# Reading part of the SSM kernel in natural layout and transposing it on PE, with DMA transposes kept for two of four segments

## The chip, the cores and the metric

The kernel runs on one core of one Trainium2 chip. The metric is the device time of one execution in microseconds (us), lower is better. Each kernel is executed several times, and most executions of a kernel agree within a per cent. Runs that are over 1.5% above the fastest of the same kernel are called slow and left out of ratios. A ratio is the mean time of one kernel's fast runs over the mean of the other's fast runs of the same rounds, so it is not quite the ratio of the medians that are quoted.

The engines are PE (matmuls), PEld (its weight loads), DVE (vector), ACT (scalar), POOL, and SP, which here only issues DMAs. The profile is one execution taken with the hardware profiler; L335 is line 335 of the program.

## The reference, cut to what matters

```python
h  = x + ln(x) * (causal_conv(kv, ssm_k) + kv * ssm_D)   # kv = shift4(k) * v
h2 = h + swiglu(ln(h))                                    # D = 640, F = 1728, S = 2048
```

The convolution over 2048 positions is done in four segments of 512. Segment p of the SSM kernel (640 channels by 512 taps) must lie with the taps on the partitions, so that PE can multiply it with a basis WG (the "G transform"). In memory `ssm_k` is `[640, 2048]`, channels first: the segment has to be transposed. D is added to tap 0.

## The kernel before

The parts that matter (`...` marks cuts). `load` and `add` enter an operation into a plan; a list scheduler then fixes the order of all engines, and each engine runs its own list strictly in that order.

```python
def gload(p, pr):            # segment p, transposed on its way in, on the SP queue
    add("SP", 2.7, lambda: nc.sync.dma_start_transpose(gT[p], A_ssm_k[:, p*MB:(p+1)*MB]), w=[f"gT{p}"], pr=pr, kb=640)
gload(0, -90)
...
add("DVE", 0.2, lambda: nc.vector.tensor_add(gT[0][0:1, 0, :], gT[0][0:1, 0, :], drow), ...)   # D

def front_tile(n, q, pr):    # k (640 KB) and v of one row tile, SP queue, then products on DVE
    load("SP", kd[:], run(r0 - 3, P), ...)
    load("SP", vb[:], vv[r0:r0 + P, :], ...)
    add("DVE", ..., lambda: nc.vector.tensor_mul(kd[:], kd[:], w4[:]), ...)
    ...

load("ACT", v of segment 0); load("ACT", WG); load("SP", k of segment 0)
g_transform(0, 9); front(0, 0)
gload(1, -30); gload(2, -20); ...; gload(3, -10)
x_transform(0, 8); pair(0, 0, 10, "first"); inverse(0, 20); ...
```

Names used below. PSUM is the memory that the matmuls write (psA and psF are its buffers); an eviction copies a result out of it. WG, WX and WI are constant bases. Front n makes kv of segment n (for segment 0 from whole-segment loads, for the others from `front_tile`). The X transform is the same as the G transform for kv; some of its results are evicted from PSUM by DVE. A pair is the complex product of one X and one G on DVE (six or eight 128x2560 operations of 1.48 us). Ten pairs, then per segment an inverse transform, a layer norm, a DMA transpose of the result (hT) and the FFN on PE.

## Time and profile before

309.1 us (median of 4 runs, 307.3 to 310.6). The profiled execution has a span of 309.8 us.

| stretch | us | what is full |
|---|---|---|
| head, to the first pair product | 0 to 41.2 | DMA engines |
| pairs of all segments | 41.2 to 240.9 | DVE (194.3 of 199.7 busy), PE nearly |
| last inverse, norm, hT | 240.9 to 258.7 | a chain over PE, ACT, DVE, POOL, DMA |
| last FFN | 258.7 to 309.8 | PE |

The table of windows shows these four stretches: start and end, its length, then busy time (and instructions) of PE, PEld, DVE, ACT and POOL, the granted PE clock, the busy share of the DMA engines, and GB/s.

```profile
41.20:240.90 199.70, 192.59 (x1128) 109.72 (x1126) 194.31 (x249) 128.37 (x249) 98.55 (x56) 0.98 0.56 146
240.90:258.70 17.80, 12.51 (x89) 7.99 (x86) 9.46 (x19) 8.39 (x18) 2.99 (x8) 0.93 0.27 65
258.70:309.80 51.10, 47.41 (x247) 23.99 (x247) 9.25 (x18) 16.54 (x28) 0.00 (x0) 0.96 0.28 75
```

Stretch 2 has DVE idle for 199.70 - 194.31 = 5.4 us only. So what starts DVE's full stretch earlier shortens the kernel, if PE can follow.

The head, in the timeline (start us, length us, engine, line, operation, result and source, count; in brackets the idle time before it and what ended it; SPq and ACTq are the issuing of DMAs):

```profile
1.23 22.30 SPq L276 DMA_TRANSPOSE wd<-in_A_ssm_k_dram  x3
...
1.67 0.45 ACTq L266 DMA_DIRECT2D hT<-in_A_v_dram  x1
...
15.34 1.23 PE L353 MATMUL psF<-hT,perm 128*128 128x320 bf16 x4 [4.07 <-DMA hT<-in_A_v_dram]
...
18.66 0.48 DVE L292 TENSOR_TENSOR wd<-wd,xln 1x640 bf16<-1x640 bf16 x1 [8.33 <-DMA wd<-in_A_ssm_k_dram]
...
23.57 5.35 SPq L276 DMA_TRANSPOSE hT<-in_A_ssm_k_dram  x1
...
25.36 3.42 PE L301 MATMUL psF<-wd,s 128*128 128x320 bf16 x24
...
27.27 0.82 DVE L373 TENSOR_TENSOR kv<-kv,rev 128x1280 bf16<-128x1280 bf16 x1
...
30.15 0.95 SPq L266 DMA_DIRECT2D k<-in_A_k_dram  x2
...
36.95 1.49 DVE L318 TENSOR_TENSOR k<-k,w 128x2560 bf16<-128x2560 bf16 x1 [3.79 <-DMA k<-in_A_k_dram]
38.35 0.82 DVE L388 CAST s<-psA 128x640 bf16<-128x640 f32 x1
...
39.23 1.22 PE L383 MATMUL psA<-kv,WX 128*128 128x320 bf16 x4 [3.38 <-DVE s L388]
...
41.22 1.48 DVE L393 TENSOR_TENSOR s<-s,s 128x2560 bf16<-128x2560 bf16 x1
```

The four transposes keep the SP queue from 1.23 to 28.92 us. Three things are late: v of segment 0 (15.3), the D add (18.7), and front 1's k loads, issued at 30.15 and 30.73.

### The profile page before, as it was taken

The page shows a single profiled execution, that of the slowest core. Times are in us where ns is not written, and L with a number is a line of the kernel's source. Part 1 is how long each engine was busy: PE and PEld are TensorE (multiplying, and loading weights), DVE is VectorE, ACT ScalarE, POOL GpSimd, SP SyncE. Part 2 cuts the span into 40 slices and gives each one's busy share as a digit, 9 for nine tenths or more (in the row PEclk, how much of TensorE's full clock was granted, in tenths as well). Part 3 has the DMA queues.
Part 4 walks back from the last instruction along what each step waited for, and adds up shares of the span by engine and source line. Part 5 has one row for each costly group of instructions (what it writes and reads, how often), then busy time and mean ns, then how long its engine had stood idle before and what let it go on. Part 6 is the DMA issues. An engine that isn't in the chain of part 4 may idle for free. (4 is left out here: it accounts for less than half of the span.)

```text
span 309.8 us, 4323 instructions
## 1 busy us (share of the span) xinstructions
PE 278.8 (90%) x1606; PEld 157.8 (51%) x1606; DVE 229.8 (74%) x302; ACT 166.1 (54%) x315; POOL 102.0 (33%) x70
## 2 busy tenths in 40 slices
PE   3389699999899998999997999999998975999995
PEld 1157457766454544655543556555455642444563
DVE  0354489999999999999996999999999660212112
ACT  5014459689775588026984491389761370555300
POOL 0000016545799936300897052049400030000000
PEclk9999969999999999999999799999999995999999
DMA  7999960639736329957363479464462032455011
GB/s 207 192 187 264 341 165 3 212 51 292 242 95 161 85 63 271 251 204 212 85 168 68 131 213 144 109 182 112 118 150 74 22 82 47 124 137 142 2 43 42
DMA packets 71769, 44.11 MB, mean 142 GB/s; under 512 B 30594, under 2 KB 69827, under 8 KB 71620
## 3 DMA queue, kind: packets, MB, share of 16 engines
q1 hardware_dynamic: 70112, 40.23, 51.7%
q10 hardware_dynamic: 1636, 3.61, 4.3%
q8 instruction: 12, 0.20, 0.3%
q14 instruction: 9, 0.07, 0.1%
HBM read 35.97 MB, written 2.62 MB: 125 GB/s over the span
## 5 line engine op out<-in xcount | busy, mean ns | idle before, releaser
L464 POOL TENSOR_SCALAR sm<-sm 128x1 f32<-128x1 f32 x32 | 56.6, 1769 | 149.2 <-ACT junk L461 142.1
L551 PE MATMUL psF<-hT,wg 128*128 128x512 bf16 x280 | 70.7, 384 | 7.7 <-DMA hT<-hl 6.8
L551 PE MATMUL psF<-hT,wu 128*128 128x512 bf16 x260 | 65.7, 384 | 0.0
L574 PE MATMUL psF<-wd,tT 128*128 128x320 bf16 x448 | 64.8, 299 | 0.8 <-ACT uc L563 0.5
L574 PEld LDWEIGHTS <-tT 128*128 128x128 bf16 x448 | 41.6, 97 | 23.7 <-issue 7.1
L556 ACT ACTIVATE sg<-psF 128x512 bf16<-128x512 f32 (+1 forms) x56 | 33.4, 597 | 27.6 <-PE psF L551 25.8
L551 PEld LDWEIGHTS <-wg 128*128 128x128 bf16 x280 | 27.5, 99 | 40.1 <-issue 10.1
L393 DVE TENSOR_TENSOR T<-s,s 128x2560 bf16<-128x2560 bf16 x32 | 47.0, 1481 | 1.0 <-ACT s L304 1.0
L393 DVE TENSOR_TENSOR s<-s,T 128x2560 bf16<-128x2560 bf16 x32 | 47.2, 1481 | 0.1
L565 DVE TENSOR_TENSOR tT<-sg,uc 128x512 bf16<-128x512 bf16 (+1 forms) x56 | 23.3, 416 | 30.7 <-ACT uc L563 30.7
L465 POOL TENSOR_TENSOR sm<-sm,mhalf 128x1 f32<-128x1 f32 x32 | 44.9, 1404 | 2.7
L563 ACT CAST uc<-psF 128x512 bf16<-128x512 f32 (+1 forms) x56 | 32.7, 585 | 17.9 <-PE psF L551 17.4
L551 PEld LDWEIGHTS <-wu 128*128 128x128 bf16 x260 | 25.6, 99 | 29.8 <-issue 1.4
L301 PEld LDWEIGHTS <-s 128*128 128x128 bf16 x256 | 25.9, 101 | 12.2 <-issue 0.8
L304 ACT CAST s<-psF 128x640 bf16<-128x640 f32 x32 | 21.9, 691 | 17.4 <-PE psF L301 17.3
L301 PE MATMUL psF<-wd,s 128*128 128x320 bf16 x192 | 29.9, 314 | 0.0
L383 PE MATMUL psA<-kv,WX 128*128 128x320 bf16 x128 | 20.7, 304 | 3.4 <-DVE s L388 3.4
L488 PE MATMUL psA<-s,WI 128*128 128x320 bf16 x128 | 20.2, 315 | 3.7 <-DVE s L393 3.6
L461 ACT ACTIVATE junk<-x,sm 128x640 bf16<-128x640 bf16 x28 | 23.4, 835 | 0.2
L579 DVE TENSOR_TENSOR o<-psF,x 128x640 bf16<-128x640 f32 x16 | 13.1, 816 | 14.0 <-PE psF L574 14.0
L460 ACT ACTIVATE junk<-x 128x640 bf16<-128x640 bf16 x28 | 20.7, 741 | 3.4 <-DVE x L511 3.0
L388 ACT CAST s<-psA 128x640 bf16<-128x640 f32 x29 | 18.9, 706 | 4.6 <-PE psA L383 4.6
(51 smaller groups left out, 222.8 us busy)
## 6 DMA issues: line engine op xcount, KB each, us to landing
k<-in_A_k_dram SPq DMA_DIRECT2D x12, 640.0 KB, 5.3
wg<-in_B_w_gate_dram SPq DMA_DIRECT2D x24, 320.0 KB, 3.1
wu<-in_B_w_up_dram SPq DMA_DIRECT2D x24, 320.0 KB, 3.7
out_dram<-o SPq DMA_DIRECT2D x16, 160.0 KB, 1.8
wd<-in_B_w_down_dram SPq DMA_DIRECT2D x1, 2080.0 KB, 9.5
v<-in_A_v_dram SPq DMA_DIRECT2D x12, 160.0 KB, 4.9
x<-in_A_q_dram SPq DMA_DIRECT2D x3, 640.0 KB, 5.1
s<-const_wg ACTq DMA_DIRECT2D x1, 1024.0 KB, 15.4
```

Source lines behind the costliest of these rows:

```text
L301: nc.tensor.matmul(ps(g)[:, h, 0:NH], WG[:, kt, ct * P:(ct + 1) * P], gT[p][:, kt, h * NH:(h + 1) * NH], start=(kt == 0), stop=(kt == 3))
L304: add("ACT", act(D), lambda g=g, ct=ct: nc.scalar.copy(r3(G[p][ct // 4][:, ct % 4, :]), ps(g)[:, :, 0:NH]), r=[g], w=[Gk[p] + "cs"[ct // 4 ...
L383: nc.tensor.matmul(ps(g)[:, h, 0:NH], WX[:, kt, ct * P:(ct + 1) * P], kv[:, base + kt, h * NH:(h + 1) * NH], start=(kt == 0), stop=(kt == 1))
L393: add("DVE", dve(n * D), lambda: f(o, a, b), r=ks(ak) + ks(bk), w=ks(ok), after=["WG0", "WG1"] if ok[:2] == "s7" else [], pr=pr)
L461: add("ACT", act(D) + 0.45, lambda: nc.scalar.activation(junk[:], src, ACT.Square, bias=s[:, 0:1], accum_out=s[:, 1:2]), r=[xk, k + "a"], ...
L464: e.tensor_scalar(s[:, 3:4], s[:, 1:2], 1.0 if vec else 1.0 / D, EPS, op0=ALU.mult, op1=ALU.add)
L465: e.tensor_tensor(s[:, 4:5], s[:, 3:4], mhalf[:], op=ALU.pow)
L551: i = nc.tensor.matmul(ps(gr)[:, which, :], w[:, kt, cc * P:(cc + 1) * P], hT[b][:, kt, :], start=(kt == 0), stop=(kt == 4))
L556: apart(gr, 0, nc.scalar.activation(sg[s][:z, :], ps(gr)[:z, 0, :], ACT.Silu))
L563: add("ACT", act(MB), lambda gr=gr, s=s, z=z, merged=merged: nc.scalar.copy(uc[s][:z, :], ps(gr)[64:128, 0, :] if merged else ps(gr)[:, 1, ...
L565: add("DVE", dve(MB), lambda c=c, s=s, z=z: TM(tT[:z, c * MB:(c + 1) * MB], sg[s][:z, :], uc[s][:z, :]), r=[f"sg{s}", f"uc{s}"], w=[f"tT{c ...
L574: nc.tensor.matmul(ps(gr)[:, h, 0:NH], tT[:z, c * MB + m * P:c * MB + (m + 1) * P], wd[:z, c, h * NH:(h + 1) * NH], start=(c == 0), stop=( ...
```

## The change

Its intent: take the slow DMA transposes away from the front. Segments 0 and 1 are loaded as they lie in memory (into buffers of the FFN that are still unused) and transposed on PE by matmuls with an identity; D is added by one-row matmuls into the same PSUM; ACT evicts. Segments 2 and 3 keep their DMA transposes, planned at 28 us or later. The diff also replaces the order pass. Cut to its core:

```diff
-    def gload(p, pr):
-        add("SP", 2.7, lambda: nc.sync.dma_start_transpose(gT[p], ...), ...)
-    gload(0, -90)
+    def gload(p, pr, q="SP"):
+        if p in TRANS:                                   # TRANS = {2: 28, 3: 28}
+            add("SP", 5.5, lambda: nc.sync.dma_start_transpose(gT[p], ...), ..., t0=TRANS[p])
+            return
+        ...                                              # kc: the FFN buffer; g, out: a PSUM group
+        load(q, kc, A_ssm_k[:, p*MB:(p+1)*MB].rearrange("(c q) t -> q c t", q=P), ...)
+        for kt in range(4):
+            ...
+            def mm(g=g, kt=kt):
+                for c in range(5):
+                    dd = p == 0 and kt == 0
+                    nc.tensor.matmul(out[:, c*P:(c+1)*P], kc[:, c, kt*P:(kt+1)*P], ident, start=True, stop=not dd)
+                    if dd:
+                        nc.tensor.matmul(out[:, c*P:(c+1)*P], ident[0:1, :], drow[:, c*P:(c+1)*P], start=False, stop=True)
+            add("PE", 0.45, mm, ...)
+            add("ACT", act(D), lambda ...: nc.scalar.copy(gT[p][:, kt, :], ...), ...)
-    add("DVE", 0.2, lambda: nc.vector.tensor_add(gT[0][0:1, 0, :], gT[0][0:1, 0, :], drow), ...)
     def order(self):
-        ... one pass of the list scheduler, ranked by hand-given priorities ...
+        first = self.forward([o["pr"] for o in self.ops])    # the same pass as before
+        for _ in range(ROUNDS):                              # ROUNDS = 3
+            last = self.forward(self.backward(...))          # ranked by latest start
+            ...                                              # keep the best by its own model
```

Other knobs that the diff adds (RES, XACT, VEC, GRACE) are set so that they do nothing.

More of the change, by code (lines that the diff above doesn't have):

```diff
@@ L60, in __init__ @@
         self.ops, self.writer, self.readers = [], {}, {}
-        self.slots = {name: [0.0] * n for name, n in pools.items()}
-        self.held = {}
+        self.pools, self.held = pools, {}
     def add(self, eng, dur, fn, r=(), w=(), pr=0, acq=None, rel=None, kb=0, after=(), t0=0.0):
@@ L73, in add @@
         i = len(self.ops)
-        self.ops.append(dict(eng=eng, dur=dur, fn=fn, deps=deps, pr=pr, acq=acq, rel=rel, kb=kb, w=list(w), t0=t0))
+        self.ops.append(dict(eng=eng, dur=dur, fn=fn, deps=deps, pr=pr, acq=acq and acq[0], rel=rel and rel[0], group=(acq or rel or (0, 0))[1], kb=kb, w=list(w), t0=t0))
         for k in r:
@@ L81, in order, with backward, forward @@
     def order(self):
+        first = self.forward([o["pr"] for o in self.ops])
+        best = first
+        for _ in range(ROUNDS):
+            last = self.forward(self.backward(first if _ == 0 else last))
+            if last[0] < best[0]:
+                best = last
+        _, out, self.held, times = best
+        for o, (s, e) in zip(self.ops, times):
+            o["start"], o["end"] = s, e
+        return out
+    def backward(self, run):
+        total, seq, _, times = run
+        ops = self.ops
+        users = [[] for _ in ops]
+        for i, o in enumerate(ops):
+            for d in o["deps"]:
+                users[d].append(i)
+        busy, late = {}, [total] * len(ops)
+        for i in sorted(range(len(ops)), key=lambda i: -times[i][1]):
+            o = ops[i]
+            end = min([late[u] - LAG.get(o["eng"], 0.12) for u in users[i]] + [total]) - (times[i][1] - times[i][0] - o["dur"])
+            taken = busy.setdefault(o["eng"], [])
+            k = len(taken)
+            for k, (a, b) in enumerate(taken):
+                if b <= end:
+                    if b <= end - o["dur"]:
+                        break
+                    end = min(end, a)
+                elif a < end:
+                    end = a
+            else:
+                k = len(taken)
+            late[i] = end - o["dur"]
+            taken.insert(k, (late[i], end))
+            taken.sort(reverse=True)
+        return late
+    def forward(self, rank):
         ops, n = self.ops, len(self.ops)
+        slots = {name: [0.0] * k for name, k in self.pools.items()}
+        spare = {name: list(range(k)) for name, k in self.pools.items()}
+        held, times = {}, [None] * n
         users = [[] for _ in range(n)]
@@ L97, in order @@
                 t = free.get(e, 0.0)
-                pick = None
+                cand = []
                 for i in l:
@@ L101, in order @@
                     if o["acq"]:
-                        sl = self.slots[o["acq"][0]]
+                        sl = slots[o["acq"]]
                         if not sl:
@@ L107, in order @@
                         s = max(s, lanes[0])
-                    key = (max(s, t), o["pr"], i)
-                    if pick is None or key < pick:
-                        pick = key
-                if pick and (best is None or pick[0] < best[0][0]):
-                    best = (pick, e)
+                    cand.append((max(s, t), rank[i], i))
+                if cand:
+                    soon = min(cand)[0] + GRACE.get(e, 0.0)
+                    pick = min((c for c in cand if c[0] <= soon), key=lambda c: (c[1], c[0], c[2]))
+                    if best is None or pick[0] < best[0][0]:
+                        best = (pick, e)
             if best is None:
@@ L118, in order @@
             if o["acq"]:
-                name, group = o["acq"]
-                sl = self.slots[name]
+                sl = slots[o["acq"]]
                 k = min(range(len(sl)), key=lambda a: sl[a])
-                idx = self.held.setdefault(("free", name), list(range(len(sl))))
-                self.held[group] = idx.pop(k)
+                held[o["group"]] = spare[o["acq"]].pop(k)
                 sl.pop(k)
@@ L135, in order @@
             if o["rel"]:
-                name, group = o["rel"]
-                self.slots[name].append(end + 0.1)
-                self.held[("free", name)].append(self.held[group])
-            o["start"], o["end"] = s, done
+                slots[o["rel"]].append(end + 0.1)
+                spare[o["rel"]].append(held[o["group"]])
+            times[i] = (s, done)
             out.append(i)
@@ L146, in order @@
                     ready.setdefault(ops[u]["eng"], []).append(u)
-        return out
+        return max(e for _, e in times), out, held, times
+ROUNDS = 3
+GRACE = {}
 RATE = 330.0
@@ L152 @@
 MOVE = "add"
+RES, XACT, VEC, TRANS = (), (), True, {2: 28, 3: 28}
 def dve(n, psum=False):
@@ L214 @@
     w4 = tl("w4", [P, 4, D])
+    ident = perm[:, 4, :]
+    kch = [tT[:, 2560 * i:2560 * (i + 1)].rearrange("p (a b) -> p a b", a=5) for i in range(2)]
     wrow = T[0:1, 0:4, :].rearrange("p a b -> p (a b)")
@@ L273 @@
     load("ACT", drow, A_ssm_D.partition_broadcast(1), ["drow"], -95.5, 5)
-    def gload(p, pr):
-        add("SP", 2.7, lambda: nc.sync.dma_start_transpose(gT[p], A_ssm_k[:, p * MB:(p + 1) * MB]), w=[f"gT{p}"], pr=pr, kb=640)
-    gload(0, -90)
+    def gload(p, pr, q="SP"):
+        if p in TRANS:
+            add("SP", 5.5, lambda: nc.sync.dma_start_transpose(gT[p], A_ssm_k[:, p * MB:(p + 1) * MB]), w=[f"gT{p}"], pr=pr, kb=640, t0=TRANS[p])
+            return
+        kc = kch[p % 2]
+        load(q, kc, A_ssm_k[:, p * MB:(p + 1) * MB].rearrange("(c q) t -> q c t", q=P), [f"kch{p % 2}"], pr, 640)
+        for kt in range(4):
+            g = ("F", "T", p, kt)
+            def mm(g=g, kt=kt):
+                out = ps(g).rearrange("p a b -> p (a b)")
+                for c in range(5):
+                    dd = p == 0 and kt == 0
+                    nc.tensor.matmul(out[:, c * P:(c + 1) * P], kc[:, c, kt * P:(kt + 1) * P], ident, start=True, stop=not dd)
+                    if dd:
+                        nc.tensor.matmul(out[:, c * P:(c + 1) * P], ident[0:1, :], drow[:, c * P:(c + 1) * P], start=False, stop=True)
+            add("PE", 0.45, mm, r=["flip", f"kch{p % 2}"] + (["drow"] if p == 0 and kt == 0 else []), w=[g], pr=pr + 50, acq=("F", g))
+            add("ACT", act(D), lambda g=g, kt=kt: nc.scalar.copy(gT[p][:, kt, :], ps(g).rearrange("p a b -> p (a b)")[:, 0:D]),
+                r=[g], w=[f"gT{p}"], pr=pr - 40, rel=("F", g))
     def wcast(t):
@@ L291 @@
         wcast(t)
-    add("DVE", 0.2, lambda: nc.vector.tensor_add(gT[0][0:1, 0, :], gT[0][0:1, 0, :], drow), r=["drow"], w=["gT0"], pr=-20)
     def g_transform(p, pr):
@@ L465, in fin @@
             e.tensor_tensor(s[:, 4:5], s[:, 3:4], mhalf[:], op=ALU.pow)
-        add("POOL", 1.5, fin, r=[k + "a", k + "b"], w=[k], pr=pr)
+            if which == 1 and n in XACT:
+                e.tensor_tensor(s[:, 5:6], s[:, 0:1], s[:, 4:5], op=ALU.mult)
+        add("POOL", 1.5 + 0.7 * (which == 1 and n in XACT), fin, r=[k + "a", k + "b"], w=[k], pr=pr)
     def scale(dst, n, q, which):
@@ L470, in scale @@
         nc.vector.tensor_scalar(dst, xin[n % 2][:, q, :], s[:, 0:1], s[:, 4:5],
-                                op0=ALU.subtract if (n, which) == (0, 2) else ALU.add, op1=ALU.mult)
+                                op0=ALU.subtract if (n, which) == (0, 2) and VEC else ALU.add, op1=ALU.mult)
     def load_x(n, pr, queue="SP"):
@@ L496, in inverse @@
                 xk = f"x{b}_{q}"
-                add("DVE", 0.24, lambda q=q, half=half: scale(xln[half][:], n, q, 1), r=[f"sm{n}{q}1", xk], w=[lk], pr=pr)
+                s = sm[n, q, 1]
+                if n in XACT:
+                    add("ACT", act(D), lambda q=q, half=half, s=s: nc.scalar.activation(xln[half][:], x[:, q, :], ACT.Identity, scale=s[:, 4:5], bias=s[:, 5:6]),
+                        r=[f"sm{n}{q}1", xk], w=[lk], pr=pr)
+                else:
+                    add("DVE", 0.24, lambda q=q, half=half: scale(xln[half][:], n, q, 1), r=[f"sm{n}{q}1", xk], w=[lk], pr=pr)
                 if half == 0:
@@ L511, in inverse @@
                 add("DVE", dve(D), lambda q=q, yb=yb: TA(x[:, q, :], x[:, q, :], yb[:]), r=[yk], w=[xk], pr=pr)
-                ln(n, q, 2, pr, n == 0)
+                ln(n, q, 2, pr, n == 0 and VEC)
                 hk = f"hl{half}"
@@ L564, in ffn @@
                     r=[(gr, 0 if merged else 1), f"sg{s}"], w=[f"uc{s}"], pr=pr - 9000, rel=("F", gr))
-                add("DVE", dve(MB), lambda c=c, s=s, z=z: TM(tT[:z, c * MB:(c + 1) * MB], sg[s][:z, :], uc[s][:z, :]), r=[f"sg{s}", f"uc{s}"], w=[f"tT{c}"], pr=pr - 9000)
+                add("DVE", dve(MB), lambda c=c, s=s, z=z: TM(tT[:z, c * MB:(c + 1) * MB], sg[s][:z, :], uc[s][:z, :]), r=[f"sg{s}", f"uc{s}"], w=[f"tT{c}"], after=["kch0", "kch1"] if n == 0 else [], pr=pr - 9000)
         for m in range(4):
@@ L570, in mm @@
                 def mm(gr=gr, m=m, c0=c0, c1=c1):
+                    if c0 == 0 and n in RES:
+                        for h in range(2):
+                            nc.tensor.matmul(ps(gr)[:, h, 0:NH], ident, xin[b][:, m, h * NH:(h + 1) * NH], start=True, stop=False)
                     for c in range(c0, c1):
@@ L574, in mm @@
                             nc.tensor.matmul(ps(gr)[:, h, 0:NH], tT[:z, c * MB + m * P:c * MB + (m + 1) * P],
-                                             wd[:z, c, h * NH:(h + 1) * NH], start=(c == 0), stop=(c == 13))
-                add("PE", 2 * (c1 - c0) * 0.137, mm, r=["wdl", "wdl2", (("F", "U", n, 13), 0)] + [f"tT{c}" for c in range(c0, c1)] + ([(gr, i - 1)] if i else []),
+                                             wd[:z, c, h * NH:(h + 1) * NH], start=(c == 0 and n not in RES), stop=(c == 13))
+                add("PE", 2 * (c1 - c0 + (i == 0 and n in RES)) * 0.137, mm, r=["wdl", "wdl2", f"x{b}_{m}", (("F", "U", n, 13), 0)] + [f"tT{c}" for c in range(c0, c1)] + ([(gr, i - 1)] if i else []),
                     w=[(gr, i)], pr=pr + 20 + m, acq=("F", gr) if i == 0 else None)
             s = m % 2
-            add("DVE", dve(D, True), lambda gr=gr, m=m, s=s: TA(r3(ot[s][:]), ps(gr)[:, :, 0:NH], r3(xin[b][:, m, :])), r=[(gr, 3), f"x{b}_{m}"], w=[f"o{s}"], pr=pr - 9000, rel=("F", gr))
+            if n in RES:
+                add("ACT", act(D), lambda gr=gr, m=m, s=s: nc.scalar.copy(r3(ot[s][:]), ps(gr)[:, :, 0:NH]), r=[(gr, 3)], w=[f"o{s}"], pr=pr - 9000, rel=("F", gr))
+            else:
+                add("DVE", dve(D, True), lambda gr=gr, m=m, s=s: TA(r3(ot[s][:]), ps(gr)[:, :, 0:NH], r3(xin[b][:, m, :])), r=[(gr, 3), f"x{b}_{m}"], w=[f"o{s}"], pr=pr - 9000, rel=("F", gr))
             r0 = n * MB + m * P
@@ L585 @@
     first_loads()
+    gload(0, -90)
     load("ACT", WX[:], WX_h.ap(), ["WX"], -25, 512, t0=8)
```

## The prediction

> **What bounds the kernel now.** Three stretches. (1) A head of 41 us: by the table of windows PE has 25.1 us of busy time in the first 40 us and DVE 15.6, while the DMA engines are full (share 0.92 to 1.16) but move only about 190 GB/s in the first 20 us, against 338 from 30 to 40. (2) From the first pair product at 41.2 us (timeline) to 246 us DVE is full (19.3 to 20.0 of every 20 us, except 17.5 at 160 to 180), PE nearly so. The chain of waits runs through the pair products for most of 185 to 236 us. (3) A tail: last inverse, layer norm and hT transposes to 258.7 us, then 47.4 us of PE alone and one eviction.
>
> **What holds the head.** In the timeline the four transposes of the SSM kernel occupy the SP queue from 1.2 to 28.9 us. Three of them land 15.4 to 17.4 us after issue. The v load, issued at 1.7, lands only at 15.3; the basis load takes 15.4 us. The Trainium skill (Advanced Engine Details and Errata, X-Bar Transpose) says that transposes are as fast as regular DMAs; this trace disagrees: a plain 640 KB load of k lands in 4.3 us. DVE waits 8.3 us (10.3 to 18.7) to add D to transposed segment 0, with the third product behind it. Front 0 ends at 28.1, the first G transform starts at 25.4, front 1's k loads are issued only at 30.
>
> **Removed:** two transposes from the start (SP occupancy 10.5+7.0 us), the D add (0.48 us) with its wait; those of segments 2 and 3 move to about 28 us.
> **Added:** two plain 640 KB loads; 40 PE transposes plus 5 one-row D products, about 0.1 us each (weight load: 97 to 101 ns), 4 to 5 us of PE, half of it where PE idles; 8 ACT evictions of 0.69 us = 5.5 us (ACT is 78% busy at 40 to 60 us).
> **Moved:** the order pass is new too: it ranks by latest start over three rounds and keeps the best by its own model, so every stage can be reordered. I expect it to put the last inverse ahead of the segment-2 down product (now 3.3 us between its matmuls, plus 0.8 us evictions on DVE) and to fill PE's 5.3 us wait for hT: 0 to 5 us gained.
>
> **Critical share.** I estimate v landing near 8 to 9 us, the kernel segment near 10, the basis near 13. Products then run 7.4 to 13.4 without a gap, front 0 ends near 18 to 19 (was 28.1), the G transform starts near 14 (was 25.4), the first pair product near 30 (was 41.2). So 9 to 11 us gained. Taken back: PE and ACT work, part of it where PE is nearly full (2 to 3 us), and late transposes colliding with loads (1 to 2 us). Reordering: -2 us, uncertain. Sum: -9 to -12.
>
> **Predicted: 298 us**, range 290 to 306. Faster by over 2%: 0.78; within 2%: 0.18; slower by over 2%: 0.04.
>
> **Signs.** Right if: v lands before 10 us; no DVE wait on the kernel transpose; first pair product near 30 us; stretch 2 keeps its 205 us (to 208); 47 us of PE after the last hT. PE busy up by 4 us, ACT by 5.5.
> **Wrong if:** the late transposes hold the SP queue so that front 1's k, v or FFN weights arrive late; PE is the real limit of stretch 2, so the early start is lost to PE waits; the new order spoils something (DVE idle over 5 us in the middle), or improves more than I think (well under 17 us from last pair product to last FFN).

## The result, and the profile after

296.8 us (median of 4 runs, 295.0 to 297.8) against 309.1 us: ratio 0.9598, 95% interval 0.9521 to 0.9674. A repetition on another occasion (below) gave 0.9549. The medians differ by 12.3 us. The profiled execution has a span of 293.2 us; it was the fastest of its kernel (295.0 us) while the profiled one of before (311.6 us) was above its median, so differences between the two profiles, 16.6 us in sum, overstate the change.

The same stretches, now bounded at 32.2, 224.95 and 244.3 us:

```profile
32.20:224.95 192.75, 185.94 (x1102) 105.40 (x1100) 189.78 (x239) 127.81 (x250) 62.31 (x56) 1.00 0.59 161
224.95:244.30 19.35, 19.30 (x136) 12.62 (x136) 11.03 (x23) 9.57 (x20) 2.99 (x8) 1.00 0.38 94
244.30:293.20 48.90, 45.27 (x248) 23.47 (x247) 10.08 (x19) 16.54 (x28) 0.00 (x0) 0.99 0.31 81
```

The head is 41.2 - 32.2 = 9.0 us shorter and stretch 2 is 6.9 us shorter. The third is 1.6 us longer, the last 2.2 us shorter. The timeline of the head:

```profile
1.23 1.15 SPq L312 DMA_DIRECT2D tT<-in_A_ssm_k_dram  x2
1.28 0.44 ACTq L312 DMA_DIRECT2D hT<-in_A_v_dram  x1
...
10.87 1.27 PE L413 MATMUL psF<-hT,perm 128*128 128x320 bf16 x4
...
14.36 16.63 SPq L312 DMA_DIRECT2D k<-in_A_k_dram  x3
...
21.49 0.82 DVE L433 TENSOR_TENSOR kv<-kv,rev 128x1280 bf16<-128x1280 bf16 x1
...
22.23 1.48 DVE L378 TENSOR_TENSOR k<-k,w 128x2560 bf16<-128x2560 bf16 x1
...
23.45 1.25 PE L361 MATMUL psF<-wd,s 128*128 128x320 bf16 x8
...
31.52 4.55 SPq L323 DMA_TRANSPOSE wd<-in_A_ssm_k_dram  x1
...
32.23 1.49 DVE L453 TENSOR_TENSOR s<-s,s 128x2560 bf16<-128x2560 bf16 x1 [1.19 <-ACT s L364]
...
36.11 2.89 SPq L323 DMA_TRANSPOSE hT<-in_A_ssm_k_dram  x1
```

Front 0 (L433) ends at 22.3 us instead of 28.1. The G transform (L361) starts at 23.45 us instead of 25.36, which is only 1.9 us earlier. But from there to the first pair product it takes 8.8 us instead of 15.9: front 1's k is issued from 14.36 us on (the first at 14.36, the second at 16.26), and DVE no longer waits for it. In this kernel the SP queue is empty and k waits for its buffers only: it leaves 0.03 us after the last matmul of front 0 that reads them (14.33 and 16.23 us). So most of the 9 us lies between the G transform and the first pair.

What the PE transposes cost, in the groups by line (busy us, mean ns of one; idle before and its releaser):

```profile
L338 ACT CAST wd<-psF 128x640 bf16<-128x640 f32 x8 | 5.2, 696 | 6.4 <-PE psF L336 4.8 <-PE psF L334 1.6
L334 PE MATMUL psF<-perm,tT 128*128 128x128 bf16 x40 | 4.1, 220 | 1.7 <-ACT s L364 0.9 <-ACT wd L338 0.8
L336 PE MATMUL psF<-xln,perm 1*128 1x128 bf16 x5 | 1.1, 226 | 0.0
```

### The profile page after: what moved, and what is told of

Its sections match the earlier page's. It is cut to its first block, busy times and chain, and to the rows that moved or that the text cites. A ratio compares the mean times of both kernels' runs of the same rounds, so it can differ in the third digit from the quotient of the medians.

```text
span 293.2 us, 4406 instructions
## 1 busy us (share of the span) xinstructions
PE 275.7 (94%) x1651; PEld 157.8 (54%) x1651; DVE 229.7 (78%) x301; ACT 169.7 (58%) x323; POOL 65.7 (22%) x70
## 4 chain that ended last, share of the span: by engine, by line
DVE 53%; PE 31%; issue 5%; ACT 4%; DMA 3%; POOL 2%; ACTq 1%; SPq 0%
DVE s L453 20%; DVE T L453 14%; PE psF L644 11%; PE psF L618 11%; DVE k L378 3%; DVE tT L632 3%; PE psA L405 3%; DMA wu<-in_B_w_up_dram 2%; PE psF L361 2%; DVE k L379 2%; PE psA L550 2%; PE psA L443 2%; DVE k L380 1%; DVE o L652 1%; DMA wg<-in_B_w_gate_dram 1%
## 5 line engine op out<-in xcount | busy, mean ns | idle before, releaser
L618 PE MATMUL psF<-hT,wg 128*128 128x512 bf16 x280 | 69.4, 379 | 0.8 <-ACT uc L630 0.8
L524 POOL TENSOR_SCALAR sm<-sm 128x1 f32<-128x1 f32 x32 | 30.2, 943 | 168.4 <-ACT junk L521 157.9
L618 PE MATMUL psF<-hT,wu 128*128 128x512 bf16 x260 | 64.5, 379 | 0.9 <-DMA wu<-in_B_w_up_dram 0.9
L623 ACT ACTIVATE sg<-psF 128x512 bf16<-128x512 f32 (+1 forms) x56 | 33.8, 603 | 45.0 <-PE psF L618 36.0
L618 PEld LDWEIGHTS <-wg 128*128 128x128 bf16 x280 | 27.2, 98 | 32.7 <-issue 2.3
L525 POOL TENSOR_TENSOR sm<-sm,mhalf 128x1 f32<-128x1 f32 x32 | 35.1, 1098 | 2.7
L361 PEld LDWEIGHTS <-s 128*128 128x128 bf16 x256 | 25.0, 97 | 11.8 <-issue 2.1
L361 PE MATMUL psF<-wd,s 128*128 128x320 bf16 x192 | 28.4, 299 | 0.9 <-ACT wd L338 0.5
L550 PE MATMUL psA<-s,WI 128*128 128x320 bf16 x128 | 18.9, 299 | 2.7 <-DVE s L453 2.7
L453 DVE TENSOR_TENSOR s<-s,s 128x2560 bf16<-128x2560 bf16 x14 | 20.5, 1480 | 1.2 <-ACT s L364 1.2
```

The lines of the kernel that those rows point to most:

```text
L361: nc.tensor.matmul(ps(g)[:, h, 0:NH], WG[:, kt, ct * P:(ct + 1) * P], gT[p][:, kt, h * NH:(h + 1) * NH], start=(kt == 0), stop=(kt == 3))
L453: add("DVE", dve(n * D), lambda: f(o, a, b), r=ks(ak) + ks(bk), w=ks(ok), after=["WG0", "WG1"] if ok[:2] == "s7" else [], pr=pr)
L524: e.tensor_scalar(s[:, 3:4], s[:, 1:2], 1.0 if vec else 1.0 / D, EPS, op0=ALU.mult, op1=ALU.add)
L525: e.tensor_tensor(s[:, 4:5], s[:, 3:4], mhalf[:], op=ALU.pow)
L550: nc.tensor.matmul(ps(g)[:, h, 0:NH], WI[:, 4 * part + ct, m * P:(m + 1) * P], a[part][:, ct, h * NH:(h + 1) * NH], start=(ct == 0), stop= ...
L618: i = nc.tensor.matmul(ps(gr)[:, which, :], w[:, kt, cc * P:(cc + 1) * P], hT[b][:, kt, :], start=(kt == 0), stop=(kt == 4))
```

## The experiments

Twelve runs in three lots. The yardstick of each lot is the kernel before, run beside it: 311.5, 310.4 and 311.2 us in the median. "First pair" is the start of the first pair product in that kernel's profile, "last pair" the end of the last one.

| run | median us | ratio to before (95%) | first pair | last pair | span |
|---|---|---|---|---|---|
| before (profile) | 309.1 | 1 | 41.2 | 240.9 | 309.8 |
| after (profile) | 296.8 | 0.9598 (0.9521 to 0.9674) | 32.2 | 224.95 | 293.2 |
| after_again | 296.6 | 0.9549 (0.9478 to 0.9620) | 33.8 | 226.5 | 294.8 |
| order_only | 313.4 | 1.0061 (0.9956 to 1.0165) | 46.1 | 242.9 | 309.6 |
| natural_old_order | 298.2 | 0.9591 (0.9521 to 0.9661) | 32.1 | 228.5 | 296.7 |
| defer_only | 306.0 | none (3 of 4 runs slow) | 43.6 | 239.1 | 307.4 |
| quiet_first | 301.0 | 0.9706 (0.9657 to 0.9755) | 34.7 | 230.0 | 298.2 |
| early_23 | 305.0 | 0.9843 (0.9779 to 0.9906) | 40.15 | 237.5 | 305.2 |
| no_d_add | 308.9 | 0.9962 (0.9884 to 1.0041) | 42.65 | 242.0 | 309.3 |
| warm_before | 308.1 | 0.9938 (0.9863 to 1.0014) | 39.0 | 237.9 | 304.9 |
| k_on_act | 313.7 | 1.0074 (1.0016 to 1.0132) | 47.0 | 247.0 | 315.6 |
| all_natural | 303.8 | 0.9784 (0.9739 to 0.9828) | 33.4 | 234.0 | 302.3 |
| nat0_idle | 299.6 | 0.9645 (0.9600 to 0.9690) | 31.4 | 227.6 | 296.3 |
| nat01_idle | 296.9 | 0.9562 (0.9518 to 0.9605) | 33.1 | 226.9 | 295.2 |

The profiled runs of `defer_only` and `k_on_act` are the slowest of their kernels (309.2 and 317.4 us) and count as slow; their profiles show where loads were held up, not what the kernel costs.

From the last pair to the end it takes 66.7 to 68.9 us in every one of these profiles, whatever was changed. The differences lie in the head and in stretch 2.

### The new order pass, alone and taken away

The change has two parts, and stretch 2, which in the kernel before has no transpose of the SSM kernel in it, shrank by 6.9 us. So the rival was that the order pass made the gain. `order_only` is the kernel before with the new pass:

```diff
 class Plan:
-    order(): one pass
+    order(), forward(), backward() of the kernel after, ROUNDS = 3
```

> The kernel before with the new order pass alone (three rounds of latest-start ranking), all four DMA transposes and the D add on DVE kept. Theory A (the 12 us come from the head, where the transposes hold the SP queue and the DMA engines): 306 to 311 us, first pair product still near 41 us. Rival B (the new order pass made most of the gain, since the stretch from first to last pair product shrank from 200 to 193 us): 302 us or less.

`natural_old_order` is the kernel after without it. With zero rounds the new pass picks as the old one did (the code says so: same start times, same ranks), so this is the old pass.

```diff
-ROUNDS = 3
+ROUNDS = 0
```

> The kernel after with the order pass set to zero rounds, which orders as the kernel before did (the same setting on the kernel before gives its instruction order exactly). Theory A: 296 to 300 us, first pair product near 32 us. Rival B: 304 us or more.

> The kernel after, unchanged, on the same chip as the other three as their yardstick: 295 to 298 us, granted clock above 0.99, while the kernel before shows 0.97 or so in its profile.

Measured: 313.4, 298.2 and 296.6 us. The pass alone gains nothing (1.0061, the interval includes 1; its median of 313.4 lies just above what theory A allowed). Without it the change keeps nearly all of its gain, 0.9591 against 0.9549 in the same rounds, so the pass is worth about 0.4% on top (0.9549 / 0.9591 = 0.9956; the four runs of each, 297.7 to 298.5 and 296.5 to 297.7 us, just touch). Its trace on stretch 2 is there: from first to last pair 199.7 us before, 196.8 with the pass alone, 196.3 with natural loads alone, about 192.7 with both, in two profiles of after. With the transposes in front, the pass's head was 46.1 us in its profile instead of 41.2, which takes its 2.9 us back.

### Clearing the queue without PE transposes

Is transposing on PE needed at all, or only the clearing of the front? `defer_only` keeps all four DMA transposes, but only segment 0's in front.

```diff
-TRANS = {2: 28, 3: 28}
+TRANS = {0: 0, 1: 28, 2: 28, 3: 28}      # D added on DVE as before, ROUNDS = 0
```

> Old order, no PE transposes at all: the DMA transpose of segment 0 alone stays in front, those of segments 1, 2 and 3 are deferred to 28 us of the plan; D is added on DVE as before. Theory C (what counts is clearing the queue of three transposes, not transposing on PE): 300 us or less, first pair product at 34 us or less. Theory D (even one DMA transpose in front holds the first loads): 303 us or more, first pair product at 36 us or more, v landing after 10 us.

Measured: 309.2, 308.4, 303.6 and 297.5 us. Neither theory is right: the runs reach from one to the other. In the profile, of the run of 309.2 us, the single transpose landed latest of all:

```profile
1.22 11.95 SPq L323 DMA_TRANSPOSE wd<-in_A_ssm_k_dram  x1
...
26.41 0.48 DVE L355 TENSOR_TENSOR wd<-wd,xln 1x640 bf16<-1x640 bf16 x1 [14.68 <-DMA wd<-in_A_ssm_k_dram]
26.85 3.25 SPq L312 DMA_DIRECT2D k<-in_A_k_dram  x2
```

It took 11.95 us to issue and landed 25 us later, with the plain loads of v, WG and WX in flight beside it. v took 20.3 us. This suggests that the company makes a transpose slow. `quiet_first` tests that: the same kernel, but all large plain loads wait, on the ACT queue, for a one-element copy of the transposed segment.

```diff
+gload(0, -200)                                   # the transpose is the first DMA
+add("ACT", 0.3, lambda: nc.scalar.copy(sg[1][0:1, 0:1], gT[0][0:1, 0, 0:1]), r=["gT0"], ...)
-load("SP",  k of segment 0)
+load("ACT", k of segment 0, r=["quiet"])         # and v, WG, perm, WX, WI: after that copy
```

> The deferred variant again (old order, DMA transpose of segment 0 in front, the others from 28 us of the plan), but the loads of k, v, the bases and q wait on the ACT queue for a one-element copy of the transposed segment, so that the transpose has the DMA engines nearly to itself. Theory F (a transpose is slow only while plain loads run beside it, and slows them): it lands within 8 us of its issue, v lands within 10 us of its own issue, first pair product at 37 to 41 us, total 300 to 304 us and all runs within 1% of each other. Rival G (a transpose of this segment is slow at the start by itself): it lands 12 us or more after issue and the total is 307 us or more.

Measured: 301.0 us, all runs within 300.0 to 301.6, ratio 0.9706. The SP queue in the timeline:

```profile
0.71 2.38 SPq L323 DMA_TRANSPOSE wd<-in_A_ssm_k_dram  x1
3.15 1.04 SPq L312 DMA_DIRECT2D v<-in_A_v_dram  x2
17.23 2.23 SPq L312 DMA_DIRECT2D k<-in_A_k_dram  x2
```

The transpose took 2.38 us to issue and landed after 4.7 us. In company, in the six kernels that begin with it, the transpose of segment 0 took 4.6 to 12.0 us to issue and 11 to 25 us to land (before 7.0 and 17.4, `warm_before` 4.6 and 11.4). v landed 6.0 us after its issue, and the first pair came at 34.7 us, earlier than the 37 to 41 that theory F expected; the rest is as F expected. So 2.9 of the 4.0 to 4.5 per cent are to be had without one transpose on PE, by keeping the transpose and the plain loads apart and clearing the queue for front 1's k (issued at 17.23, as soon as its buffer is free). The other part is probably that PE transposes let the loads start at once: the first large plain load of this variant goes out at 5.4 us. No run separates that.

### What exactly is late

`no_d_add` removes the DVE wait for transposed segment 0, by leaving D out (a wrong result).

```diff
-add("DVE", 0.2, lambda: nc.vector.tensor_add(gT[0][0:1, 0, :], gT[0][0:1, 0, :], drow), ...)
```

> The kernel before without the addition of D on DVE (wrong result on purpose): DVE no longer waits 8.3 us for transposed segment 0 with the third product behind it. If that wait was the cause of the late front: 304 us or less, first pair product at 37 us or less. If the front is late because v and the bases land late anyway: 307 to 312 us, the DVE wait moving to the products that need v, first pair product at 39 us or later.

Measured: 308.9 us, first pair at 42.65. Front 0 ended at 21.9 us in this profile, 6.2 us earlier than before, and nothing came of it: with the four transposes still ahead in the SP queue, front 1's k was issued at 31.16 us, DVE waited 3.59 us for it, and the first pair came 11.5 us after its issue. An early front 0 is worth nothing while the queue holds k back.

Three profiles with four transposes in front and the old order can be lined up in this way. Front 0 ended at 28.1 us (before), 21.9 (`no_d_add`) and 22.1 (`warm_before`, below). k was issued at 30.15, 31.16 and 28.01, DVE waited for it in each, and the first pair came 11.1, 11.5 and 11.0 us later. In these, the first pair follows k's issue and not front 0.

`early_23` is the kernel after with its two remaining transposes right behind the first plain loads.

```diff
-TRANS = {2: 28, 3: 28}
+TRANS = {2: 0, 3: 0}                             # and gload(2), gload(3) called right after gload(0), gload(1)
```

> The kernel after with the two remaining DMA transposes (segments 2 and 3, which nothing needs before 45 us) issued right behind the plain loads of segments 0 and 1, in the crowded first microseconds. Theory F (interference between transposes and plain loads): v or the bases land later than in the kernel after (6.3 and 7.7 us), first pair product at 37 us or later, total 301 us or more. Rival H (only the work that waits for a transposed segment suffers, and the loads behind the transposes in their queue): first pair product below 35 us, total 296 to 299 us.

Measured: 305.0 us, first pair at 40.15. The timeline shows how:

```profile
2.32 13.65 SPq L323 DMA_TRANSPOSE wd<-in_A_ssm_k_dram  x1
...
16.01 5.46 SPq L323 DMA_TRANSPOSE hT<-in_A_ssm_k_dram  x1
...
21.59 0.50 SPq L312 DMA_DIRECT2D k<-in_A_k_dram  x1
21.70 0.82 DVE L433 TENSOR_TENSOR kv<-kv,rev 128x1280 bf16<-128x1280 bf16 x1
...
29.05 1.49 DVE L378 TENSOR_TENSOR k<-k,w 128x2560 bf16<-128x2560 bf16 x1 [6.52 <-DMA k<-in_A_k_dram]
...
31.32 0.82 DVE L448 CAST s<-psA 128x640 bf16<-128x640 f32 x1
...
32.19 2.36 PE L443 MATMUL psA<-kv,WX 128*128 128x320 bf16 x8 [4.50 <-DVE s L448]
```

This is the size that theory F expected, but most of it came by way of the queue, as in rival H. v landed 9.0 us after issue (6.3 and 8.4 in the two profiles of after), yet the matmuls that need it began at 10.89 us, as after (10.87), and front 0 (L433) ended at 22.5 us, as after (22.3). Nothing waits for segments 2 and 3 here. Front 1's first k load, however, was issued at 21.6 us behind the transposes instead of 14.4, although its buffer was free at 14.5. It also took longer to land, 7.4 us instead of 4.9, with a transpose still in flight; that part is interference, as in theory F. DVE waited 6.52 us for k, the X eviction stood behind that product, PE waited 4.50 us for the buffer, and the first pair came 7.9 us later. These are the same links as in the last lines of the head before. About 2 of the 7.9 us came on top: after its idle time PE had a granted clock of 0.50 from 32.1 to 36.5 us, and two groups of eight matmuls took 2.36 and 2.34 us instead of 1.25. (The plan was made anew for this variant, so PE's order differs a little too: the G transform began at 24.8 us instead of 23.45.)

`k_on_act` tries the converse: the kernel before, with those k and v loads on the ACT queue, so that they do not stand behind the transposes in the SP queue.

```diff
-load("SP", kd[:], run(r0 - 3, P), ...); load("SP", vb[:], ...)
+load(..., via="ACT" for n == 1, q in (0, 1))     # the plan, and so PE's and DVE's orders, unchanged
```

> The kernel before with one thing changed: the first two k and v tile loads of front 1 go out on the ACT queue, so that they no longer stand behind the four transposes in the SP queue (PE and DVE instruction orders identical to before). Theory K (the head ends late because these loads, issued at 28 to 30 us, keep the product of front 1 and, behind it in DVE's order, the last X evictions waiting): no DVE wait on k over 1 us, first pair product at 37 us or earlier, total 303 to 307 us. Rival L (the transposed segment 0 and the slowed loads bound the head by themselves): first pair product at 39 us or later, total 308 us or more.

Measured: 313.7 us, ratio 1.0074, first pair at 47.0 in the profile of its slowest run: not faster, if anything slower. It does not test theory K, because it brought a fault of its own. DVE no longer waited for k, but the second k load got out of the ACT queue only at 32.7 us, and the evictions of the G transform stood behind it in ACT's order; ACT then had been idle for 17 us:

```profile
32.71 0.33 ACTq L266 DMA_DIRECT2D k<-in_A_k_dram  x1
33.09 0.68 ACTq L266 DMA_DIRECT2D WI<-const_wi  x1
33.81 1.29 ACT L304 CAST s<-psF 128x640 bf16<-128x640 f32 x2 [16.98 <-issue]
```

Why it left so late can be read from the landings. The moved loads take nothing from the transposes, and yet three of the four left just when a transpose landed (the other v load followed the first): the first transpose landed at 19.58 us and the first v load left at 19.61; the second at 21.93, the first k load at 22.04; the fourth at 32.62 (23.18 and 9.4 us), the second k load at 32.71. In the trace all DMAs of the SP and ACT queues of this program signal their landing on eight semaphores, used over and over, and a DMA's instruction waits until the last DMA on its semaphore has landed, whichever queue that one was in. So another queue did not free these loads from the transposes. (`no_d_add` shows it too: the load of q in the ACT queue left at 25.29, when the second transpose had landed at 25.27, and ACT stood idle for 12.7 us until 26.29.)

A load cannot be moved to a queue whose engine also computes without looking at what stands behind it, and at what it waits for itself. What this run leaves open is how much of the head before the k loads alone explain, with the transposes still in front.

### The granted clock

The profile before shows a mean granted clock of 0.972, after 0.999. Could that be the gain? `warm_before` puts 98 useless matmuls into the three idle times of PE after which the clock was near 0.5.

```diff
+def keep_warm(k, one=False):
+    for i in range(k): nc.tensor.matmul(psA[...][:, 1, NH:512], perm[:, 0, :], ..., start=True, stop=True)
+# 28 before the last group of the first X transform, 20 in the third inverse, 50 before the last FFN
```

> The kernel before with 98 idle matmuls of 192 columns (into unused PSUM columns) placed in front of the three matmuls before which PE stood idle and after which the profile shows a granted clock of about 0.5: the last group of the first X transform (28), the second half of the third inverse (20), the first up matmul of the last segment (50). Theory A (the clock is a small part): the profile's clock rises to 0.985 or more, the last FFN's up and gate part shortens from 31.5 to about 29.3 us, and the total falls by 2 to 3 us, to 306 to 309. Rival E (the clock is most of the gain): 302 us or less.

Measured: 308.1 us, ratio 0.9938, interval 0.9863 to 1.0014: at most about 1.4%, and not clear of nothing. Its clock was 0.992. Where the last FFN begins, before:

```profile
252.00:258.70 6.70, 1.41 (x10) 0.62 (x8) 1.63 (x3) 1.44 (x4) 1.29 (x3) 0.82 0.56 122
258.70:263.00 4.30, 4.26 (x11) 1.50 (x12) 0.00 (x0) 0.60 (x1) 0.00 (x0) 0.50 0.01 4
263.00:267.00 4.00, 4.00 (x20) 1.83 (x19) 0.85 (x2) 2.27 (x4) 0.00 (x0) 0.98 0.31 84
```

and with the useless matmuls:

```profile
255.70:259.00 3.30, 3.23 (x15) 1.53 (x17) 0.31 (x1) 1.18 (x2) 0.00 (x0) 1.00 0.00 0
259.00:263.00 4.00, 4.00 (x20) 1.80 (x19) 0.54 (x2) 2.34 (x4) 0.00 (x0) 1.00 0.53 135
```

After an idle time of 5.33 us PE got half its clock and did 11 matmuls in 4.3 us instead of 20 in 4.0. The Trainium skill (TensorE: Matmul & The Clock Gate, What's actually happening) puts the clock at half after an idle window of about 3.4 us; the trace agrees as far as it goes, 5.33 us being longer than that. The last FFN took 47.5 us before (258.7 to 306.2) and 45.6 us in this run (255.7 to 301.3), so one episode costs about 2 us. The new order has the last FFN follow other matmuls without a gap, so the kernel after has this gain too. It is a small part of the 12 us. (In this execution the head was also 2.2 us shorter than in the profile of before. The four transposes took less time to issue, to 26.8 us instead of 28.9, and front 1's k left 2.1 us earlier; 28 of the idle matmuls stand in the head as well, but after k had left.)

### Other divisions between PE and DMA

Three attempts to beat the kernel after: no DMA transpose of the SSM kernel, one segment on PE and three DMA transposes in the quiet stretch, and two segments on PE with the two DMA transposes earlier.

```diff
-TRANS = {2: 28, 3: 28}
+TRANS = {}                                # all_natural
+TRANS = {1: 17, 2: 20, 3: 23}             # nat0_idle
+TRANS = {2: 17, 3: 20}                    # nat01_idle
```

> The kernel after with all four segments read in natural layout and transposed on PE, no DMA transpose of the SSM kernel at all. It adds 40 more PE transposes (about 4 us of PE) and 8 ACT evictions (5.5 us). If the two late DMA transposes still cost something (they hold the SP queue from 31.5 to 39 us): 293 to 296 us. If they cost nothing and PE is the limit: 297 to 301 us.

> The new order pass, but only segment 0 in natural layout; the DMA transposes of segments 1, 2 and 3 are planned at 17 to 23 us, into the stretch in which the DMA engines of the kernel after stand idle (25 to 30 us: share 0.00). Saves 20 PE transposes and 4 evictions. If transposes cost nothing when no plain load runs beside them: 292 to 296 us, transposes landing within 8 us. If the loads of front 1 (k, v) still collide with them: 298 us or more, a DVE wait on k.

> The kernel after with its two remaining DMA transposes planned at 17 and 20 us instead of 28, so ahead of the third k load of front 1 in the SP queue and in the idle stretch of the DMA engines. If they are harmless there: 294 to 297 us, the same as after or up to 1% faster. If they delay the loads behind them: 298 us or more.

Measured: 303.8, 299.6 and 296.9 us. None beats the kernel after. `all_natural` lies outside both ranges expected of it; it is 7 us slower than after, more than the 4 us of PE that it adds: first to last pair takes 200.6 us instead of 192.7, and its profile has DVE waiting 3.9 us for G evictions of ACT near 79 us. `nat01_idle` is the kernel after within its noise.

`nat0_idle` had the earliest first pair of all, 31.4 us, and lost it in stretch 2 (196.2 us); I did not follow up where. Its total lies in the range of the collision, but DVE did not wait for k, and the first transpose landed after 16.5 us instead of the 8 expected. It had company again: the load of the basis WI (512 KB), issued at 17.39 us, landed only at 32.6. The line of the DMA view (KB, us to landing), then the table of windows before and after that landing (the last two columns are DMA share and GB/s):

```profile
WI<-const_wi ACTq DMA_DIRECT2D x1, 512.0 KB, 15.2
...
22.00:24.00 2.00, 2.00 (x15) 1.45 (x15) 1.97 (x2) 1.27 (x2) 0.00 (x0) 1.00 1.33 115
...
26.00:28.00 2.00, 2.00 (x17) 1.43 (x16) 2.00 (x4) 1.07 (x2) 0.00 (x0) 1.00 1.41 146
...
32.00:34.00 2.00, 1.98 (x16) 1.28 (x15) 2.00 (x2) 1.93 (x5) 0.00 (x0) 1.00 0.96 216
```

and the kernel after, where plain loads fill the engines, and later, from 35.5 us, the two transposes alone:

```profile
5.00:10.00 5.00, 2.53 (x9) 1.08 (x9) 2.76 (x2) 1.99 (x4) 0.00 (x0) 1.00 1.08 358
10.00:15.00 5.00, 5.00 (x30) 3.20 (x28) 4.16 (x5) 1.29 (x2) 0.00 (x0) 1.00 1.04 402
...
35.50:37.50 2.00, 1.13 (x14) 0.84 (x13) 1.93 (x3) 2.00 (x5) 0.88 (x2) 1.00 1.20 268
```

With full engines, plain loads move 358 to 402 GB/s, transposes alone 216 to 268, and transposes with one plain load among them 115 to 146, less than either kind alone. By my estimate from these shares and rates, a transposed byte keeps the engines busy 1.5 to 1.7 times as long as a plain one; the rest is what they cost each other. The head before, with four transposes among its plain loads, moved 190 GB/s with full engines, which fits. What in the DMA engines makes the company so slow is not shown.

## Why the prediction was right or wrong

The total (298 predicted, 296.8 measured, range 290 to 306) and the direction were right, and the cause named, the transposes in front, is confirmed: the change keeps its gain without the new order pass, and putting two transposes back in front (`early_23`) costs 8 us. Several steps of the sum were not right, and they cancelled; that 298 lies so near to 296.8 is in part luck.

- **First pair near 30 us, 9 to 11 us gained in the head:** measured 32.2 and 33.8 us in two profiles, 7.4 to 9.0 us gained. Nearly right in size, at the low end.
- **v lands before 10 us, no DVE wait on the transposed kernel:** both right (issued at 1.28, 6.3 us to landing; no such wait).
- **Front 0 ends near 18 to 19 us, G transform starts near 14, and so the first pair comes early:** this step failed. Front 0 ended at 22.3 and the G transform started at 23.45 us. I had costed DVE's products but not PE's order, in which the matmuls of front 0, the transposes and the first X groups stand ahead of the G transform, with PE full from 10 to 20 us. The G transform came only 1.9 us earlier than before. Most of the 9 us arose after it, because front 1's k loads were issued 15.8 us earlier (14.36 instead of 30.15). I had read their issue at 30 us from the trace and listed it, but did not follow what waits for k: a product in DVE's order, with the X evictions behind it. `no_d_add` (front 0 6.2 us earlier, k still late, nothing gained) and `early_23` (front 0 unchanged, k late, 7.9 us lost) show that k's issue is what counts, in those variants; for the kernel before itself the direct test (`k_on_act`) failed, and the three profiles lined up above are the evidence. Front 0 does have a part, by a link that I had not seen: k's buffers are freed by its matmuls, at 14.33 us instead of 20.30. So of the 15.8 us, about 6.0 are those of front 0 and 9.8 those of the queue, and a clear queue alone could not have brought k before 20.3.
- **"Stretch 2 keeps its 205 us (to 208)", taken back 3 to 5 us there:** wrong in sign. I measured it to 246 us then; from first to last pair it went from 199.7 to 192.75 us. DVE's busy time in it fell by 4.5 us, because that much work moved out: 2.1 us into the head (16.75 to 18.81 us busy) and 2.4 us behind the last pair; DVE's idle time fell from 5.4 to 3.0 us. About half of the 7 us is the order pass.
- **Reordering: the last inverse goes ahead of the segment-2 down product, PE's 5.3 us wait for hT is filled, -2 us:** the wait was filled (the last FFN follows matmuls directly), but from last pair to last FFN it takes 19.35 us instead of 17.8. The gain seems to have come out as clock: the last FFN at full clock, 45.3 us of PE busy time instead of 47.4, where I had predicted 47 us. As a whole the pass is worth about 0.4%.
- **PE busy up by 4 us, ACT by 5.5:** the added groups were sized right (PE 4.1 and 1.1 us, ACT 5.2 us). But PE's total fell from 278.8 to 275.7 us, probably since matmuls at half clock count as busy for longer (the mean clock rose from 0.972 to 0.999); ACT's rose by 3.6 us.

The prediction set transposes of 15.4 to 17.4 us against a plain load of 4.3 us. That mixed the transpose with its company: with nearly nothing beside it, it landed after 4.7 us (`quiet_first`), and in the same company the plain loads of v and WG took 13.6 and 15.4 us too.

What stays open: the spread of a transpose in company. The same DMAs in front gave v after 7.4 to 14.2 us in five kernels that begin as before does, and `defer_only` reached from 297.5 to 309.2 us. No run here shows what decides it.

## What to carry to other kernels

Read a DMA queue as a list with an order: ask of each slow DMA not only who waits for its data, but which loads stand behind it (or wait for its semaphore, from another queue), when their buffers come free, and what waits, in the in-order engines, for those. A transposing DMA that shares the first microseconds with bulk loads can cost several times its own time (25.2 us to landing against 4.7 here). Loading plainly and transposing on PE brought 4.0 to 4.5% here, and one transpose alone in front, the others later, 2.9%. Transposing all four segments on PE, more than the front needs, cost 7 us of that again.

## What the Trainium skill lacked or had wrong

- Advanced Engine Details and Errata, X-Bar Transpose: "TRN2 transpose DMAs are as fast as regular DMAs", with 350 to 400 GB/s expected. In this shape (640 rows of 512 bf16 elements, rows 4 KB apart) transposes alone moved 216 to 268 GB/s with full engines, plain loads 358 to 402. One transpose of 640 KB with nearly nothing beside it landed in 4.7 us, the first plain load of 640 KB in 4.2 to 5.1 us.
- DMA: Bandwidth & Descriptors, Rules for kernel authors: a transpose next to ordinary DMAs "needs nothing". For correctness the runs agree. For time they do not: beside bulk loads the same transpose took 11 to 25 us to land instead of 4.7, and 4.6 to 12.0 us to issue instead of 2.4; two transposes and one plain load together moved 115 to 146 GB/s. No page that I read has this.
- DMA: Bandwidth & Descriptors, Issuing engines are not separate DMA queues: spreading DMAs over issuing engines saves only issue time, "usually small relative to the DMA itself". Here it was not small: the four transposes occupied the SP queue for 27.7 us in all (1.23 to 28.92), and what stood behind them was late.
- SBUF — State Buffer, SBUF: two separate sides, describes the port that DVE and POOL share as an exclusive lock. It has no example as long as this one. In the kernel before, a 128x1 operation on POOL that takes 0.19 us elsewhere took 17.39 us while DVE was full, and DVE then waited 2.53 us for the result of the next one. That the lock is the cause is not shown: spans on POOL are rough, and in `natural_old_order`, with DVE as full (191.0 of 196.3 us), the same operation never took more than 3.2 us.
